# Two transposes in one visit, a block-diagonal inverse product, padded tiles and a reordered opening in a fused attention and gated-MLP kernel

## Chip, cores and metric

The kernel runs on one core of a Trainium2 chip. Five engines run their own queues: TensorE (PE; its weight loads are listed as PEld), VectorE (DVE), ScalarE (ACT), GpSimd (POOL) and SyncE (SP), which here issues the transfers. The metric is the device time of one launch in microseconds (us); lower is better. Matmuls read SBUF, the on-chip memory of 128 partitions, and write PSUM, eight banks of 2 KB per partition.

## What is computed

Landmark (Nyström) attention over 8 batches of 8 heads, followed by RMS normalisation and a gated MLP whose weights arrive in float64. Cut to what matters:

```python
q_lm = q.reshape(B, H, 32, 18, D).mean(axis=3)      # B=8, H=8, S=576, D=64
k_lm = k.reshape(B, H, 32, 18, D).mean(axis=3)
A, Bm, C = sm(q, k_lm), sm(q_lm, k_lm), sm(q_lm, k)  # softmax rows
Z = Bm.T / (norm1(Bm) * norminf(Bm) + 1e-6)
for _ in range(6):
    Z = 2 * Z - Z @ Bm @ Z
x = (A @ Z @ C @ v)                                  # -> 4608 tokens x 512
xn = x / sqrt(mean(x * x) + 1e-6) * rms_g
out = (silu(xn @ w_gate) * (xn @ w_val)) @ w_out     # d_ff = 1536
```

## The kernel before, in words

**The MLP** is the bulk of the work. For each batch it runs twice, over the first six blocks of 128 hidden columns ("early" weights) for batches 0 to 7, then over the last six ("late" weights) for batches 0 to 7. One such pass is 144 matmuls into `psg` and `psv` (moving operand: `an`, the normalised activations split into a high and a low part, 288 columns) and then 72 or 90 matmuls into `pso` (stationary: `h`; moving: `whio`/`wloo` early, `lhio`/`lloo` late, 512 columns). The weights are folded with each batch's attention values: `mix_weights` multiplies `WT` (from the inverse) with a pair of decoded weight blocks `wgv` into `pM`, and ACT and DVE split that into `Mhi` and `Mlo`. There are three pairs for each half.

**Decoding** turns a float64 block into float32: two ACT operations (L175, L178), two on DVE (L180, L183); out-weights need two more, `whio` on ACT and `wloo` on POOL. The first six raw blocks land in the `h` tiles, the later ones in a ring of three buffers, so that the transfer of the tenth block waits until the seventh has been decoded. A pair takes four blocks, gate and value of two hidden blocks.

**Attention** of the next batches is cut into short pieces, "visits", that stand between MLP matmuls at positions written in the code (`until(chunk, n)` counts MLP matmuls; `rest` and `steady` hold the tables). For each batch and each of two groups of four heads: landmark sums `lmT` (L380, DVE), `front` (scores `sC`, `sA`), `soften`, `turn` (transposes of `E` into `sE`, `sF`, copied to `ET`, `EL` by ACT) and `values` (`pCV`). Then come the inverse (`newton_start`, first product `p`, six steps `pn`, L668), `newton_weights` (eight small products `pW` with 32x32 blocks, copied twice side by side to `W`), `newton_values` (two transposes `pT`, scaled to `WT`), and `second` (`pO`, squares, `pss`, `pms`, the reciprocal root in small DVE steps, `an`). PSUM has four banks for the MLP (`pg`) and four for attention (`pa`). Each engine runs its queue in order; the order is made by the builder from these positions and priorities.

**The opening** (batch 0's attention, with no MLP work yet, then the first pass, in which batch 1's attention and the decoding of all early weights run too) has its own pieces: `opening`, `first_inverse`, `first_second`, and the head of `steady`. Batch 1's first `front` stands after batch 0's `pms` and first `pM`; batch 1's sums for its second group stand ahead of the second pair's decoding. In the first pass a pair is mixed in the middle of the pair before it (`very`).

**Layout.** `gsb`, the norm weights, takes 16 bytes a partition and is followed on the left side of SBUF by `WT`, the `h` tiles, early weights, `Mhi`, `Mlo`, `an` and others. In the built program these start 32 bytes past a multiple of 64; the late out-weights (on the right side) start at multiples of 64.

## Time and profile before

| | |
|---|---|
| Median of 3 runs | 837.14 us (836.75 to 837.6) |
| Profiled execution | 836.84 us |
| its span, first to last instruction | 834.7 us |
| TensorE busy | 800.4 us, 96% |
| VectorE busy | 490.9 us, 59% |
| ScalarE busy | 350.9 us, 42% |
| GpSimd busy | 71.0 us, 9% |
| Mean granted TensorE clock | 0.973 |

In the profile, a row of the timeline gives start, duration, engine, line, operation, output and inputs, and in brackets how long the engine sat idle before it and what ended that. A granted clock of 1.00 is 2.4 GHz and of 0.50 is 1.2 GHz. Matmul durations overlap, so that pitch is read from start to start. A float32 matmul that isn't a transpose shows as two instructions.

### The profile page before, as it was taken

Reading aid. Unit: us, or ns where it says so; the run is one execution under the profiler, and the core shown is the slowest. Engines: PE = TensorE matmul, PEld = TensorE weight load, DVE = VectorE, ACT = ScalarE, POOL = GpSimd, SP = SyncE. Lnnn points to the kernel's source line nnn. Section 1 sums busy time; section 2 is a strip of 40 time slices with the busy share of each in tenths; the row PEclk is TensorE's granted clock in tenths of the full one; section 3 lists DMA queues with packets and bytes.
Section 4 is the critical chain, followed back from the end, with each engine's and each line's share of the span. In section 5 each row is a group of like instructions: output and inputs, shape, how many; then the busy total and the mean of one; then the engine's idle time right before and its main releaser. Section 6 shows DMA issues by size and latency. Waiting matters only on the chain.

```text
span 834.7 us, 17401 instructions
## 1 busy us (share of the span) xinstructions
PE 800.4 (96%) x7192; PEld 630.3 (76%) x7192; DVE 490.9 (59%) x1095; ACT 350.9 (42%) x749; POOL 71.0 (9%) x97
## 2 busy tenths in 40 slices
PE   7756999999999999999999999999999999999998
PEld 4334667877878778777787879797979797979796
DVE  7787976856768748668584945242524252425241
ACT  4557644535445444445464844141414141414140
POOL 1012411020020200201110110000000000000000
PEclk8579999999999999999999999999999999999999
DMA  9756452250440612503436510413141304130202
GB/s 326 242 172 216 143 191 89 84 195 15 144 136 2 228 65 92 188 2 109 140 114 229 176 71 13 145 54 118 22 146 53 121 22 147 50 124 14 88 14 75
DMA packets 41054, 95.49 MB, mean 114 GB/s; under 512 B 4112, under 2 KB 17424, under 8 KB 38928
## 3 DMA queue, kind: packets, MB, share of 16 engines
q1 hardware_dynamic: 40976, 94.39, 33.4%
q8 instruction: 56, 0.92, 0.5%
q14 instruction: 22, 0.18, 0.1%
HBM read 66.06 MB, written 28.31 MB: 113 GB/s over the span
## 4 chain that ended last, share of the span: by engine, by line
PE 86%; DVE 5%; DMA 4%; ACT 2%; POOL 1%; issue 1%; SPq 1%; ACTq 0%; DVEq 0%
PE pso L109 35%; PE psg L109 19%; PE psv L109 18%; PE pM L109 6%; PE pn L109 2%; DMA wrawg<-in_moe_w_gate_dram 2%; PE pO L109 1%; PE sC L109 1%; PE pss L109 1%; DMA wrawv<-in_moe_w_val_dram 1%; PE pCV L109 1%; DMA qk<-in_k_dram 1%; PE sE L112 1%; DVE wgv L180 1%; SPq L152 0%
## 5 line engine op out<-in xcount | busy, mean ns | idle before, releaser
L109 PE MATMUL pso<-whio,h 128*128 128x512 f32 x432 | 140.7, 397 | 2.1 <-ACT ob L848 2.1
L109 PE MATMUL pso<-lhio,h 128*128 128x512 f32 x432 | 138.7, 396 | 0.0
L316 DVE TENSOR_TENSOR s<-s,psv 128x288 f32<-128x288 f32 x192 | 85.9, 450 | 60.0 <-PE psv L109 59.3
L315 ACT ACTIVATE s<-psg 128x288 f32<-128x288 f32 x192 | 78.7, 410 | 89.9 <-PE psg L109 89.5
L268 ACT CAST Mhi<-pM 128x512 fp32r<-128x512 f32 x96 | 51.4, 591 | 137.6 <-PE pM L109 137.2
L323 ACT CAST h<-s 128x576 fp32r<-128x576 f32 x96 | 64.6, 673 | 86.2 <-DVE s L316 86.2
L109 PEld LDWEIGHTS pso<-whio,h 128*128 128x128 f32 x432 | 81.6, 189 | 24.3 <-issue 4.2
L109 PEld LDWEIGHTS pso<-lhio,h 128*128 128x128 f32 x432 | 81.0, 187 | 24.8 <-DVE obl L911 5.9
L324 DVE TENSOR_TENSOR h<-s,h 128x576 fp32r<-128x576 f32 x96 | 72.7, 758 | 44.5 <-ACT h L323 44.3
L109 PE MATMUL psg<-an,Mhi 128*128 128x288 f32 x384 | 85.4, 307 | 4.8 <-ACT s L315 3.4
L911 DVE TENSOR_TENSOR obl<-obl,pso 128x512 f32<-128x512 f32 x36 | 24.8, 688 | 107.6 <-PE pso L109 107.4
L109 PE MATMUL pso<-wloo,h 128*128 128x512 f32 x216 | 86.4, 400 | 0.0
L109 PE MATMUL pso<-lloo,h 128*128 128x512 f32 x216 | 85.2, 395 | 0.0
L109 PE MATMUL psv<-an,Mhi 128*128 128x288 f32 x384 | 84.4, 303 | 0.0
L270 DVE TENSOR_TENSOR Mlo<-pM,Mhi 128x512 fp32r<-128x512 f32 x94 | 60.3, 683 | 37.5 <-ACT Mhi L268 37.5
L109 PE MATMUL psg<-anl,Mhi 128*128 128x288 f32 x384 | 81.7, 301 | 0.6 <-DVE Mlo L270 0.6
L109 PE MATMUL psv<-anl,Mhi 128*128 128x288 f32 x384 | 79.1, 294 | 0.0
L109 PEld LDWEIGHTS psg<-an,Mhi 128*128 128x128 f32 x384 | 62.3, 191 | 17.5 <-issue 6.7
L109 PEld LDWEIGHTS psg<-anl,Mhi 128*128 128x128 f32 x384 | 60.9, 188 | 15.5 <-issue 12.6
L109 PEld LDWEIGHTS psv<-an,Mhi 128*128 128x128 f32 x384 | 61.6, 188 | 6.1 <-issue 2.2
L109 PEld LDWEIGHTS psv<-anl,Mhi 128*128 128x128 f32 x384 | 61.5, 188 | 0.0
L109 PE MATMUL psg<-an,Mlo 128*128 128x288 f32 x192 | 58.5, 305 | 0.0
(138 smaller groups left out, 1249.8 us busy)
## 6 DMA issues: line engine op xcount, KB each, us to landing
qk<-in_q_dram SPq DMA_DIRECT2D x16, 576.0 KB, 4.8
qk<-in_k_dram SPq DMA_DIRECT2D x16, 576.0 KB, 5.8
ad<-an SPq DMA_DIRECT2D x8, 1152.0 KB, 5.1
pd<-ob SPq DMA_DIRECT2D x36, 256.0 KB, 2.4
anl<-ad SPq DMA_DIRECT2D x8, 1152.0 KB, 5.1
obl<-pd SPq DMA_DIRECT2D x36, 256.0 KB, 2.7
out_dram<-obl SPq DMA_DIRECT2D x36, 256.0 KB, 2.0
vt<-in_v_dram SPq DMA_DIRECT2D x16, 512.0 KB, 4.1
```

The costliest lines, as they stand in the source:

```text
L109: tc.keep_in_program_order(nc.tensor.matmul(*args, **kw))
L112: tc.keep_in_program_order(nc.tensor.transpose(*args))
L180: nc.vector.scalar_tensor_tensor(w, w, 3, wtail, op0=ALU.logical_shift_left, op1=ALU.bitwise_or)
L268: nc.scalar.copy(hi[:, g], ps[g])
L270: nc.vector.tensor_sub(lo[:, g], ps[g], hi[:, g].bitcast(F32))
L315: silu["last"] = nc.scalar.activation(s[:, cols], banks[0], AF.Silu).ins
L316: nc.vector.tensor_mul(s[:, cols], s[:, cols], banks[1])
L323: nc.scalar.copy(h[:, 0, TAIL:], s)
L324: gated[b, f0 // NF1, 2 * n + i] = nc.vector.tensor_sub(h[:, 1, TAIL:], s, h[:, 0, TAIL:].bitcast(F32))
L911: nc.vector.tensor_add(ob, ob, ps)
```

## The change

1. **Tiles.** `gsb` is padded to 64 bytes. In the built program the left-side tiles then start at multiples of 64; those on the right side stay where they were.
2. **Inverse product.** `newton_weights` and `newton_values` become one visit. GpSimd copies the four 32x32 blocks of each group into a block-diagonal 128x128 matrix `blocks` (four copies a batch); two matmuls with it give `pW` straight (for `W`, now half as wide) and two give it turned, which DVE scales to `WT`. `VF` is written by two DVE instructions instead of one.
3. **Reciprocal root.** Eight DVE steps instead of ten.
4. **Visits of batches 2 to 7.** Both `turn`s in one visit, both `values` and the first inverse product in the next, `ET` and `EL` with two buffers; positions moved.
5. **Opening.** Batch 1's first sums stand ahead of `WT`; its first `front` stands between batch 0's `pms` and the first `pM`; one more weight block is decoded before `an`; batch 1's second sums stand behind the decoding of two pairs; the next pair is mixed half a block later, behind 12 more MLP matmuls; the remaining positions moved.

```diff
-    gsb = cst.tile([P, NK], F32, name="gsb")
+    gsb = cst.tile([P, 16], F32, name="gsb")[:, :NK]
     WT = cst.tile([P, B, NK, 2 * M], F32, name="WT")
+    blocks = cst.tile([P, 2, P], F32, name="blocks")
+    nc.gpsimd.memset(blocks, 0.0)
...
             for i in range(2):
-                if very and i and n + 1 < NPAIR:
-                    mix_weights(wts, b, pairs[n + 1])
-                    yield 1.1
                 s = mp.tile([P, S], F32, name="s", tag="s", bufs=2)
                 for e in range(2):
+                    if very and i and e and n + 1 < NPAIR:
+                        mix_weights(wts, b, pairs[n + 1])
+                        yield 1.1
...
             yield from until(*next(at))
-            values(b, 0)
-            turn(b, 1)
+            if b > 1:
+                turn(b, 0)
+                turn(b, 1)
+                yield 1.1, 0.0
+                yield from until(*next(at))
+                values(b, 0)
+                values(b, 1)
+            else:
+                values(b, 0)
+                turn(b, 1)
+                yield 1.5, 0.0
+                yield from until(*next(at))
+                values(b, 1)
...
-            front(1, 0, fixed["an", 0].ins)
-            load_qk(2, 0)
-            yield 1.3, 0.0
-            sums(1, 1, fixed["mx", 1, 0].ins)
-            yield from until(0, 24)
+            yield from until(0, 12)
             turn(1, 0)
             yield 0.65, 0.0
-            yield from until(0, 36)
+            yield from until(0, 37)
+            sums(1, 1, early.last)
+            yield from until(0, 46)
             front(1, 1)
...
-            at = [46, 58, 70] + [78 + 8 * n for n in range(6)] + [126, 132, 138, n_gv + 4, n_gv + 10, n_gv + 18]
+            at = [54, 66, 78] + [84 + 7 * n for n in range(6)] + [126, 136, n_gv + 4, n_gv + 10, n_gv + 18]
...
-                enter = [n_gv + n for n in ((4, 28, 36, 48, 54, 66) if c else (16, 40, 46, 56, 62, 70))]
+                enter = [n_gv + n for n in ((4, 30, 44, 50, 62) if c else (16, 40, 52, 60, 70))]
...
-                after = [7 * n for n in range(7)] + [48, 54, 68, 86, 96]
+                after = [7 * n for n in range(6)] + [48, 56, 68, 86, 96]
...
+            for h in range(4):
+                nc.gpsimd.tensor_copy(blocks[rows(h), :, rows(h ^ 1)], Bs[rows(h)])
+            return BT, den
...
-            for g in range(2):
-                for h in range(4):
-                    r = rows(rho(g, h))
-                    mm(pW[rows(pos(g, h)), g], Bs[r, g, :], VF[r, g, :], start=True, stop=True)
-            W = sm.tile([P, 2, 2, D], F32, name="W", tag="W", bufs=2)
-            fixed[b] = nc.vector.tensor_copy(W, pW.unsqueeze(2).broadcast_to([P, 2, 2, D]))
+            for g in range(2):
+                mm(straight[:, g], blocks[:, g], VF[:, g, 0], start=True, stop=True)
+            for g in range(2):
+                mm(turned[:, g], VF[:, g].rearrange("p a d -> p (a d)"), blocks[:, g], start=True, stop=True)
+            W = sm.tile([P, 2, D], F32, name="W", tag="W", bufs=1)
+            fixed[b] = nc.vector.tensor_copy(W, straight)
...
-            for n, took in enumerate(second(0)):
-                yield took
-                if n == 2:
-                    low_parts = mix_weights(early, 0, 0, True)
-                    yield 1.1, 0.0
+            parts = second(0)
+            yield next(parts)
+            sums(1, 0, fixed[0].ins)
+            yield next(parts)
+            yield from parts
+            front(1, 0, fixed["r1", 0].ins, fixed["an", 0].ins)
+            load_qk(2, 0)
+            yield 1.3, 0.0
+            low_parts = mix_weights(early, 0, 0, True)
+            yield 1.1, 0.0
             low_parts()
```

How the order changes is shown at three places. The first is DVE in the opening. Before, behind the score transposes `tA` of batch 1's first group (numbers behind a name tell tiles apart; `wgv_664` is the second pair):

```order
L440 STREAM_TRANSPOSE tA<-sA 128x288 x2
L380 TENSOR_REDUCE lmT<-qk_353 128x64 x2
L180 SCALAR_TENSOR_TENSOR wgv_664<-wgv_664,wrawg_356 128x4x128
L433 TENSOR_SCALAR ss<-ss 128x1
L434 TENSOR_SCALAR ss<-ss 128x1
L183 SCALAR_TENSOR_TENSOR wgv_664<-wrawg_356,wgv_664 128x4x128
L435 RECIPROCAL rs<-ss 128x2
L316 TENSOR_TENSOR s<-s,psv 128x288
```

Now, at the end of the same decoding (`wgv_554` is the second pair, `wgv_755` the third; the second pair's first block was decoded ahead of `an`):

```order
L182 SCALAR_TENSOR_TENSOR wgv_554<-wgv_554,wrawv_366 128x4x128
L319 TENSOR_TENSOR s<-s,psv 128x288
L327 TENSOR_TENSOR h_713<-s,h_713 128x576
L185 SCALAR_TENSOR_TENSOR wgv_554<-wrawv_366,wgv_554 128x4x128
L182 SCALAR_TENSOR_TENSOR wgv_755<-wgv_755,wrawg_368 128x4x128
L185 SCALAR_TENSOR_TENSOR wgv_755<-wrawg_368,wgv_755 128x4x128
L383 TENSOR_REDUCE lmT<-qk_357 128x64 x2
L273 TENSOR_TENSOR Mlo<-pM,Mhi 128x512 x2
```

The landmark sums `lmT` of batch 1's second group moved from ahead of the second pair's decoding to behind it and behind the third pair's first block.

The second place is TensorE in the second pass, where batch 2's inverse ends. Before:

```order
L109 MATMUL psg<-an,Mhi 128x288 x2
L109 MATMUL psg<-an,Mlo 128x288
L109 MATMUL pW<-VF,Bs 32x64 x8
L109 MATMUL psv<-an,Mhi 128x288 x2
L109 MATMUL psv<-an,Mlo 128x288
L109 MATMUL psv<-an,Mhi 128x288 x2
L109 MATMUL psv<-an,Mlo 128x288
L112 MATMUL pT<-ident,W 128x128 x2
L109 MATMUL pM<-wgv_743,WT 32x512 x8
```

Now:

```order
L111 MATMUL psg<-an,Mhi 128x288 x2
L111 MATMUL psg<-an,Mlo 128x288
L111 MATMUL psv<-an,Mhi 128x288 x2
L111 MATMUL psv<-an,Mlo 128x288
L111 MATMUL psv<-an,Mhi 128x288 x2
L111 MATMUL psv<-an,Mlo 128x288
L111 MATMUL pW<-VF,blocks 128x64 x2
L111 MATMUL pW<-blocks,VF 128x128 x2
L111 MATMUL pM<-wgv_755,WT 32x512 x8
```

The two visits `pW` and `pT` became one, of four full-width matmuls, just ahead of `pM`.

The third place is ACT at the end of the first pass, around the copies `ob` that free the banks of `pso`. Before:

```order
L739 ACTIVATE sq<-pO 128x288 x2
L424 ACT_TABLE_LOAD
L424 ACTIVATE E,ss<-sC,mx 128x288
L774 CAST an<-AT 128x576 x2
L424 ACTIVATE E,ss<-sC,mx 128x288
L428 ACTIVATE eb,ss<-sC,mx 128x32
L848 COPY ob<-pso 128x512 x2
L268 CAST Mhi<-pM 128x512 x2
```

Now:

```order
L191 CAST whio_1221<-w_1216 128x512
L775 CAST an<-AT 128x576 x2
L859 COPY ob<-pso 128x512 x2
L427 ACT_TABLE_LOAD
L427 ACTIVATE E,ss<-sC,mx 128x288 x2
L431 ACTIVATE eb,ss<-sC,mx 128x32
L271 CAST Mhi<-pM 128x512 x2
```

The `ob` copies moved from behind batch 2's exponentials `E` to ahead of them.

## Rows read from the trace of the kernel before

**Rows 1.** Busy time by stage (engine busy us and count, then TensorE's granted clock).

```profile
40.00:60.00 20.00, 10.78 (x97) 6.19 (x89) 17.68 (x42) 10.80 (x20) 3.09 (x1) 0.76 0.41 144
60.00:80.00 20.00, 13.67 (x213) 10.24 (x205) 15.35 (x45) 13.87 (x28) 3.72 (x4) 0.93 0.70 228
80.00:100.00 20.00, 19.48 (x234) 14.40 (x222) 17.22 (x33) 14.06 (x30) 9.16 (x8) 0.94 0.44 137
...
140.00:800.00 660.00, 658.90 (x5689) 530.48 (x5688) 370.20 (x804) 268.94 (x576) 44.85 (x68) 1.00 0.29 99
```

**Rows 2.** TensorE's waits: total us, times, longest us.

```profile
PE pM L109 <- DVE wgv L183: 7.5, 1, 7.5
...
PE psg L109 <- ACT s L315: 3.4, 2, 2.9
PE pso L109 <- ACT ob L848: 2.1, 1, 2.1
```

**Rows 3.** Timeline from 36 to 60 us: start, us, engine, line, operation [idle before].

```profile
42.07 1.07 ACT L276 CAST Mlo<-pM 128x512 fp32r<-128x512 f32 x2 [0.40 <-PE pM L109]
...
48.88 2.57 DVE L380 TENSOR_REDUCE lmT<-qk 128x64 f32<-128x1152 f32 x2
...
51.37 0.68 DVE L180 SCALAR_TENSOR_TENSOR wgv<-wgv,wrawg 128x512 int32<-128x512 int32 x1
...
56.32 3.09 POOL L322 CAST h<-h 128x128 fp32r<-128x128 f32 x1 [37.79 <-DVE h L324]
...
57.97 0.68 DVE L183 SCALAR_TENSOR_TENSOR wgv<-wrawv,wgv 128x512 int32<-128x512 int32 x1
...
58.71 1.96 PE L109 MATMUL pM<-wgv,WT 64*32 64x512 f32 x16 [7.52 <-DVE wgv L183]
```

**Rows 4.** Timeline from 60 us, VectorE's two waits for weights.

```profile
61.76 0.69 DVE L180 SCALAR_TENSOR_TENSOR wgv<-wgv,wrawv 128x512 int32<-128x512 int32 x1 [2.50 <-ACT wgv L178]
...
65.84 0.69 DVE L180 SCALAR_TENSOR_TENSOR wgv<-wgv,wrawg 128x512 int32<-128x512 int32 x1 [2.65 <-ACT wgv L178]
```

**Rows 5.** Timeline, two out-matmuls: the first of all, and one that waited.

```profile
97.05 0.40 PE L109 MATMUL pso<-whio,h 128*128 128x512 f32 x1
...
115.08 0.50 PE L109 MATMUL pso<-whio,h 128*128 128x512 f32 x1 [2.08 <-ACT ob L848]
```

**Rows 6.** Chain of work, two long runs of out-matmuls: start, us, what and count.

```profile
475.98 20.42 PE pso L109 x90
...
810.12 20.97 PE pso L109 x90
```

**Rows 7.** Timeline of batch 5's attention visits, TensorE, between out-matmuls.

```profile
276.87 0.60 PE L112 MATMUL sE<-ident,E 128*128 128x128 f32 x4
277.30 0.27 PE L112 MATMUL sF<-ident,E 128*64 128x128 f32 x1
...
287.20 0.48 PE L109 MATMUL pso<-whio,h 128*128 128x512 f32 x1
287.52 0.39 PE L109 MATMUL pso<-wloo,h 128*128 128x512 f32 x1
```

**Rows 8.** Timeline, TensorE, matmuls around a pW and around a pT visit.

```profile
94.02 0.29 PE L109 MATMUL psv<-an,Mlo 128*128 128x288 f32 x1
...
94.72 0.29 PE L109 MATMUL psg<-an,Mlo 128*128 128x288 f32 x1
...
249.78 0.30 PE L109 MATMUL psg<-an,Mlo 128*128 128x288 f32 x1
...
250.19 0.29 PE L109 MATMUL psg<-an,Mlo 128*128 128x288 f32 x1
...
251.15 0.29 PE L109 MATMUL psv<-an,Mlo 128*128 128x288 f32 x1
```

**Rows 9.** Tile h: durations min/median/max of the tail copies on GpSimd.

```profile
L322 POOL CAST h<-h x48: 289/293/3088, 56.3 to 772.6; 128x128 fp32r<-128x128 f32 x48
```

More of the change, by code (lines that the diff above doesn't have):

```diff
@@ L130, in __init__ @@
             self.place = place
-            self.spots, self.ahead, self.after, self.then = spots, ahead, None, None
+            self.spots, self.ahead, self.after, self.then, self.last = spots, ahead, None, None, None
             self.raws, self.gv, self.out = {}, {}, {}
@@ L182, in load_next @@
                 )
-            nc.vector.scalar_tensor_tensor(
+            last = nc.vector.scalar_tensor_tensor(
                 w, whead, -0x80000000, w, op0=ALU.bitwise_and, op1=ALU.bitwise_or
             )
+            self.last = last.ins
             if nm == "o":
@@ L385, in sums, with front @@
                     )
-        def front(b, g, after=None):
+        def front(b, g, after=None, late=None):
             nt, lmT, qk = state[b], lms.pop((b, g)), loaded.pop((b, g))
@@ L447, in front @@
             if b:
-                tail(after)
+                tail(late or after)
             return tail
@@ L531, in rest @@
             yield from until(*next(at))
-            values(b, 0)
-            turn(b, 1)
+            if b > 1:
[11 more added lines that the diff above has]
+                values(b, 1)
             if b + 1 < B:
                 load_v(b + 1, 0)
-            yield 1.5, 0.0
-            yield from until(*next(at))
-            values(b, 1)
-            if b + 1 < B:
                 load_v(b + 1, 1)
@@ L552, in rest @@
             with tc.high_priority():
-                newton_weights(b, inverse[2])
-            yield 0.4, 0.0
-            yield from until(*next(at))
-            with tc.high_priority():
-                newton_values(b)
-            yield 0.3, 0.0
+                newton_weights(b)
+            yield 0.6, 0.0
             stage["newton"] = stage["wt"] = b
@@ L603, in steady @@
                 yield from until(c, enter[1])
-                turn(b, 0)
-                yield 0.65, 0.0
-                yield from until(c, enter[2])
                 front(b, 1)
@@ L611, in steady @@
                 inverse = newton_start(b)
-                after = [7 * n for n in range(7)] + [48, 54, 68, 86, 96]
-                yield from rest(b, inverse, [(c, n) for n in enter[3:]] + [(c + 1, n) for n in after])
+                after = [7 * n for n in range(6)] + [48, 56, 68, 86, 96]
+                yield from rest(b, inverse, [(c, n) for n in enter[2:]] + [(c + 1, n) for n in after])
         def bmm(lt, rhs, n, nm):
@@ new lines, in newton_weights @@
+            for g in range(2):
+                mm(turned[:, g], VF[:, g].rearrange("p a d -> p (a d)"), blocks[:, g], start=True, stop=True)
+            W = sm.tile([P, 2, D], F32, name="W", tag="W", bufs=1)
+            fixed[b] = nc.vector.tensor_copy(W, straight)
+            fixed["WT", b] = nc.vector.tensor_mul(
+                WT[:, b],
+                turned.rearrange("p g (j n) -> p (g j) n", j=2),
+                gsb.unsqueeze(2).broadcast_to([P, NK, 2 * M]),
+            )
+            state[b]["W"] = W
@@ L706, in newton @@
                 yield 0.45, NP
[L707 to L710 removed]
+            newton_weights(b)
+            yield 0.6, WW
             stage["wt"] = b
@@ L735, in second @@
                         r = rows(pos(g, h))
-                        mm(po[2 * g + h // 2][half(h)], W[r, g, 0, :], ATs[g][r, cols], start=True, stop=True)
+                        mm(po[2 * g + h // 2][half(h)], W[r, g, :], ATs[g][r, cols], start=True, stop=True)
                 sq = ap.tile([P, NK, HS], F32, name="sq", tag="sq", bufs=2)
@@ L757, in second @@
             r2 = sm.tile([P, NB], F32, name="r2", tag="r2")
-            ri = r1.bitcast(I32)
-            nc.vector.tensor_single_scalar(ri, ms.bitcast(I32), 1, op=ALU.logical_shift_right)
-            nc.vector.tensor_scalar(ri, ri, -1, 0x5F3759DF, op0=ALU.mult, op1=ALU.add)
-            for c in (1.0, RS):
-                nc.vector.tensor_mul(r2, r1, r1)
-                nc.vector.scalar_tensor_tensor(r2, r2, c, ms, op0=ALU.mult, op1=ALU.mult)
-                nc.vector.scalar_tensor_tensor(r2, r2, -10.0 / 3.0, r2, op0=ALU.add, op1=ALU.mult)
-                last = nc.vector.scalar_tensor_tensor(r1, r2, 5.0, r1, op0=ALU.add, op1=ALU.mult)
+            nc.vector.tensor_scalar(
+                r1.bitcast(I32), ms.bitcast(I32), -0.5, 0x5F3759DF, op0=ALU.mult, op1=ALU.add
+            )
+            nc.vector.tensor_mul(r2, r1, r1)
+            nc.vector.scalar_tensor_tensor(r2, r2, -0.5, ms, op0=ALU.mult, op1=ALU.mult)
+            nc.vector.scalar_tensor_tensor(r1, r2, 1.5, r1, op0=ALU.add, op1=ALU.mult)
+            nc.vector.tensor_mul(r2, r1, r1)
+            nc.vector.tensor_mul(r2, r2, ms)
+            nc.vector.scalar_tensor_tensor(r2, r2, -10.0 / 3.0, r2, op0=ALU.add, op1=ALU.mult)
+            last = nc.vector.scalar_tensor_tensor(r1, r2, 5.0, r1, op0=ALU.add, op1=ALU.mult)
+            fixed["r1", b] = last
             if b == 0:
@@ L814, in nystrom_moe_kernel @@
         new_state(0)
+        new_state(1)
         if WN0:
@@ L832, in decode @@
             yield from early.stream(WAIT0, NEAR)
+            while ("sums", 1) not in fixed:
+                yield -0.3
+            early.then = fixed["sums", 1].ins
+            yield from early.stream(WAIT0, 1)
         early.ahead, early.after = 2, fixed["eb", 0, 1].ins
```

41 lines of the change are left out of this document (14 added, 27 removed).

## The prediction, made before the changed kernel was run

> **What bounds the kernel now.** I read the busy time by stage first. From 140 to 800 us TensorE is busy 658.90 of 660 us at a granted clock of 1.00 (2.4 GHz) [rows 1]: there nothing that another engine does can be won back, and only the number, the pitch or the gaps of TensorE's own instructions count. Between 40 and 100 us it is busy 10.78, 13.67 and 19.48 of 20 us, that is 16.07 us idle, and the granted clock is 0.76, 0.93 and 0.94 [rows 1]. In the same 60 us DVE is busy 17.68 + 15.35 + 17.22 = 50.25 us, so DVE has 9.75 us left: it is the engine that nearly binds the opening. The second view is TensorE's waits: one of 7.5 us for the second weight pair's last decoding step (L183), 2.9 of 3.4 us for `s` on ACT, 2.1 us for a copy `ob` on ACT [rows 2]. The third is the timeline there: DVE first sums landmarks (`lmT`, 2.57 us), begins to decode the second pair at 51.37 and writes its last step at 57.97; TensorE starts `pM` at 58.71 [rows 3]. Then DVE waits 2.50 and 2.65 us itself for further raw weights [rows 4]. So the kernel is a steady part set by TensorE's pitch, and an opening set by DVE's order.
>
> **Opening.** The wait of 7.5 us ends with DVE's row of work. Three things leave that row: the `lmT` pair, 2.57 us [rows 3]; the two steps of the pair's first block, which now fall into DVE's idle time ahead of `an`, 2 x 0.68 = 1.36; and one step of the third pair that stood ahead of the second pair's last, another 0.6 (a step lasts 0.68 [rows 3], and they follow one another a little closer). That is 4.5 us. Against it, the second cast of `an` now stands on ACT behind the two `Mlo` casts (1.07 us together [rows 3]), and DVE's `an` and the decoding wait for that: 4.5 - 1.1 = 3.4 us. Ahead of the second pair's `pM` there are now 12 more matmuls `psg`/`psv`, which did not wait for it and used to come after it: 3 such in 250.19 - 249.78 = 0.41 us [rows 8], so 12 take 1.6. TensorE is then 3.4 + 1.6 = 5.0 us ahead at the same work. The moved `lmT` does not come back as a loss, since it lands where DVE waited 2.50 us [rows 4]. The raw blocks behind it are asked for sooner, because the ring's buffers come free sooner; the other DVE wait, 2.65 us [rows 4], and TensorE's wait of 2.9 us for `s`, which lies behind it on ACT [rows 2], then shrink. I take 2.0 us of that, since ACT still has the same casts and decodings to do. Together -7.0 us at the first `pso`, which was at 97.05 [rows 5]. The bounds: -9.75, all of DVE's idle time [rows 1], and -2, if ACT's queue eats the 12 matmuls and the early block. Earlier `front`, shorter root and the earlier sums are inside this: they only move DVE steps of a fixed total and lie beside the casts that `an` waits for.
>
> **End of the first pass.** The `ob` copies now precede batch 2's exponentials, so the wait of 2.08 us at 115.08 [rows 5] goes. What is late next is batch 2's second `front`, placed 6 out-matmuls earlier; its `lmT` pair (2.57 us [rows 3]) stands behind `an` of batch 1 on DVE, whereas the four banks and the whole queue of TensorE stand behind that `front`. I put the new wait at 2.1 us, so that the two cancel; bounds 0 and 2.6, by the same row.
>
> **Batches 2 to 7.** Two visits in place of three. After a visit the next `pso` starts 287.52 - 287.20 = 0.32 us after the first one behind it [rows 7], where two follow each other in 20.42 / 90 = 0.227 [rows 6]: 0.09 us lost on leaving; I take as much for entering, 0.18 a batch, 6 x 0.18 = -1.1. The doubled `ET` copies on ACT have some 12 out-matmuls of cover, 2.7 us; if ACT's `tA` steps eat it, the cost is at most one more such copy, for which a 512-column step of 0.68 us [rows 3] is the nearest row: up to 0.7 a batch, kept for the range.
>
> **Inverse product.** Before, the `pW` visit costs 251.15 - 250.19 - 0.41 = 0.55 and `pT` 94.72 - 94.02 - 0.41 = 0.29 [rows 8], 0.84 together. Now there are four full-width float32 matmuls, which show as eight instructions, each with a 128-column weight load. Nearest are the transposes `sE`: four in 277.30 - 276.87 = 0.43 [rows 7], 0.11 each. Eight take 0.86, with 0.09 for leaving 0.95: +0.1 a batch, for seven batches inside the stream +0.7. The halved `W` and the second `VF` step are on DVE, which has time left there. Bounds -0.3 and +1.5 for all.
>
> **Tiles.** Early out-matmuls run at 20.42 / 90 = 0.2269 us, late ones at 20.97 / 90 = 0.2330 [rows 6], with the same shape and clock. What differs is the place: early `h` and `whio` both start 32 bytes past a multiple of 64, late `h` still does but `lhio` starts at a multiple. After the change all start at multiples. If it is the disagreement of the two operands that costs, the late ones drop to the early pitch: 2 x 324 = 648 late matmuls x 0.0061 = -3.9 us, and nothing else changes. I take this, because the one pair of rows that shows a difference has equal offsets on the fast side. The other ends are in the rivals. The Trainium skill speaks against any gain: "SBUF — State Buffer", section "Operand start alignment", asks only that an operand start at a multiple of its element size and names no better start. By that the term would be 0 and the sum 3.9 us higher; no run here shows it yet, and the two pitches have then another cause.
>
> **The sum.** 836.84 (profiled execution) - 7.0 + 0 - 1.1 + 0.7 - 3.9 = 825.5. The median stands 0.3 above the profiled execution, so 825.8.
>
> **Rivals.** *Pitch unchanged*: the late pitch comes from something else (copies, stores), the padding does nothing: 829.7. For it speaks that the late half also has other users of the memory; against it that 90 undisturbed matmuls at the end keep it [rows 6]. *All matmuls gain*: the slow thing is a start off 64 bytes anywhere: 648 early `pso` and 2304 `psg`/`psv` gain up to 0.0061 each, 18 us more: 808 to 822. Against it: early `pso`, off 64 on both sides, is the faster one. *A start at 64 bytes is the slow one* (slower side): what marks the slow late rows is a moving operand at a multiple of 64. Then early `pso` go to the late pitch, 648 x 0.0061 = +4.0, the late ones stay, and `psg`/`psv`, whose `an` moves to such a start too, may gain as much: 2304 x 0.0061 = +14. That gives 836.84 - 7.4 + 4.0 = 833.7 without them and 847.8 with them; it is slower than before once `psg`/`psv` cost over 0.0015 us more each. For it speaks the same pair of rows [rows 6], which can't tell the two readings apart. *The opening's gain is lost*: the four `blocks` copies run on GpSimd among DVE's decoding, and one GpSimd copy took 3.09 us at 56.32 between such steps [rows 3] where the median is 0.293 [rows 9]; with the casts queued behind `Mlo` this eats the 7 us: 832.8, up to 835.4 if the new `front` wait comes on top. Against it: `blocks` are wanted only six steps later. The Trainium skill's "SBUF — State Buffer", section "Who interferes with whom", says that a DVE instruction with two SBUF inputs blocks a GpSimd one that reads SBUF; the copy's 3.09 us agrees.
>
> **Chances.** The sum as it stands 0.45 (821 to 830); pitch unchanged 0.21 (826 to 834); all gain 0.07; slow start 0.13 (half of it above 838); opening lost 0.10 (832 to 837); none of these 0.04. The range 815 to 836 leaves out most of "all gain" and of the slow start. About 0.2% is what a measurement of this kernel can tell from no change, 835.5 to 838.8 here: faster 0.83, same 0.07, slower 0.10, from the upper half of the slow start and the worst of the others.
>
> **What would show it.** Right: the wait for L183 falls from 7.5 us to about 2 or less, the first `pso` stands near 90, late runs of 90 `pso` take 20.4 us, and no row of `psg` changes. Wrong: a 90-run early at 20.97; `psg` groups of 3 over 0.41; a wait of `sC` for `lmT` over 3 us near 115; `pCV` waits for `ET` in every batch; or a first `pso` after 94, which would leave the opening to ACT's queue.

## The result, and the profile after

The changed kernel takes 828.37 us (median of 4 runs, 828.0 to 829.41); beside it the kernel before took 836.94 us (median of 4, 834.67 to 837.6). The ratio is 0.9904, with an interval from 0.9884 to 0.9925: 8.6 us faster by the medians, where 11.3 were forecast. The profiled execution took 828.0 us with a span of 826.2 us, 8.5 less than the span before (834.7).

Where the 8.5 us came from is seen by cutting both spans at the same four points of the program. In the trace they are the first out-matmul `pso`, the 73rd (the first of the second pass), the first one of the late half, and the last one. All are read at the start of the matmul.

| stretch | before, us | after, us | difference | forecast |
|---|---|---|---|---|
| start to the first `pso` | 97.05 | 94.46 | -2.59 | -7.0 |
| first `pso` to the second pass's first | 62.29 | 59.02 | -3.27 | 0 |
| from there to the first late `pso` | 360.11 | 360.93 | +0.82 | -0.4 |
| late half, to the start of the last `pso` | 311.23 | 307.75 | -3.48 | -3.9 |
| sum | 830.68 | 822.16 | -8.52 | -11.3 |

The sum is near the forecast, but only the term of the late half is: the opening gave little over a third of what was expected, the end of the first pass gave 3.3 us that were not expected at all, and the third stretch lost 0.8 us where 0.4 were to be gained. That the errors partly cancel (4.4, 1.2 and 0.4 us too little, 3.3 too much) is luck.

The busy time by stage, which answers [rows 1] (columns: stretch, us; busy us and count of TensorE, its weight loads, VectorE (DVE), ScalarE (ACT), GpSimd (POOL); granted clock, DMA share, GB/s):

```profile
40.00:60.00 20.00, 15.30 (x131) 9.43 (x124) 15.05 (x40) 9.78 (x22) 0.62 (x1) 0.75 0.41 146
60.00:80.00 20.00, 16.33 (x221) 11.66 (x220) 19.93 (x51) 16.17 (x30) 6.89 (x9) 0.76 0.74 233
80.00:100.00 20.00, 19.42 (x216) 14.30 (x209) 19.75 (x33) 14.56 (x31) 9.10 (x9) 0.98 0.44 149
140.00:800.00 660.00, 658.89 (x5627) 536.76 (x5627) 369.11 (x797) 267.55 (x577) 49.85 (x88) 1.00 0.29 99
```

From 140 to 800 us nothing has changed in kind: TensorE is busy 658.89 of 660 us. In the opening it is now busy 4.5 us more between 40 and 60 us and 2.7 more from 60 to 80, there in part because the granted clock is lower (0.76 for 0.93) and the same matmul lasts longer. But look at DVE: it has 4.95 us left in the first of these stretches, more than before (2.32), and 0.07 and 0.25 us in the other two. The idle time of DVE that the prediction wanted to use from 60 us on is used up; what is left stands ahead of 60 us.

TensorE's waits, which answer [rows 2] (us in total, times, longest):

```profile
PE pM L111 <- DVE wgv L185: 1.9, 1, 1.9
...
PE psg L111 <- ACT s L318: 1.4, 2, 0.9
```

The wait for the second pair's last decoding step (L183 before, L185 now) went from 7.5 to 1.9 us, the wait for `s` from 3.4 to 1.4, and the wait for `ob` is gone. A reader who stops here would call the opening's forecast right. The timeline says otherwise. Rows that answer [rows 3] and [rows 5] (start, us, engine, line, operation, then the idle time before it and what ended it):

```profile
46.26 0.67 ACT L775 CAST an<-AT 128x576 fp32r<-128x576 f32 x1 [6.58 <-DVE AT L773]
46.84 1.06 ACT L271 CAST Mhi<-pM 128x512 fp32r<-128x512 f32 x2
...
48.00 1.08 ACT L279 CAST Mlo<-pM 128x512 fp32r<-128x512 f32 x2
...
48.97 0.67 ACT L775 CAST an<-AT 128x576 fp32r<-128x576 f32 x1
49.68 0.76 DVE L776 TENSOR_TENSOR an<-AT,an 128x576 fp32r<-128x576 f32 x1 [1.77 <-ACT an L775]
...
55.36 0.46 DVE L319 TENSOR_TENSOR s<-s,psv 128x288 f32<-128x288 f32 x1 [1.03 <-PE psv L111]
...
56.93 0.46 DVE L319 TENSOR_TENSOR s<-s,psv 128x288 f32<-128x288 f32 x1 [0.52 <-PE psv L111]
...
58.71 1.09 PE L111 MATMUL pM<-wgv,WT 64*32 64x512 f32 x16 [1.89 <-DVE wgv L185]
...
94.46 0.40 PE L111 MATMUL pso<-whio,h 128*128 128x512 f32 x1
```

The second pair's `pM` starts at 58.71 us, exactly where it started before [rows 3]. The shorter wait only means that TensorE did something else meanwhile: the 12 `psg`/`psv` that used to come behind. The second cast of `an` stands behind both `Mhi` and `Mlo` on ACT, DVE waits for it, and its second `an` ends at 49.68 + 0.76 = 50.44 us. Before, both stood one behind the other and ended at 45.74 + 1.43 = 47.17:

```profile
45.74 1.43 DVE L775 TENSOR_TENSOR an<-AT,an 128x576 fp32r<-128x576 f32 x2
```

The chain of work, two long runs of out-matmuls (start, us, what, count), for [rows 6]:

```profile
470.94 20.42 PE pso L111 x90
...
802.13 20.44 PE pso L111 x90
```

The late runs are now as fast as the early ones: 20.44 / 90 = 0.2271 us a matmul, where it was 20.97 / 90 = 0.2330. The early runs kept 20.42. This is what the forecast for the tiles said, almost to the digit.

### The profile page after: what moved, and what is told of

The parts are those of the page before. It is cut to its first block, busy times and chain, and to the rows that moved or that the text cites. A ratio compares the mean times of both kernels' runs of the same rounds, so it can differ in the third digit from the quotient of the medians.

```text
span 826.2 us, 17288 instructions
## 1 busy us (share of the span) xinstructions
PE 797.0 (96%) x7112; PEld 635.1 (77%) x7112; DVE 492.9 (60%) x1087; ACT 349.6 (42%) x749; POOL 78.2 (9%) x130
## 4 chain that ended last, share of the span: by engine, by line
PE 88%; DVE 4%; DMA 4%; ACT 2%; issue 1%; SPq 1%; ACTq 0%; DVEq 0%
PE pso L111 36%; PE psg L111 19%; PE psv L111 18%; PE pM L111 6%; DMA wrawg<-in_moe_w_gate_dram 2%; PE pn L111 2%; PE sC L111 2%; PE pO L111 1%; PE pCV L111 1%; PE pss L111 1%; DMA qk<-in_k_dram 1%; SPq L154 1%; PE sE L114 1%; PE pW L111 1%; DVE h L327 1%
## 5 line engine op out<-in xcount | busy, mean ns | idle before, releaser
L111 PE MATMUL pso<-lhio,h 128*128 128x512 f32 x432 | 136.5, 392 | 0.0
L327 DVE TENSOR_TENSOR h<-s,h 128x576 fp32r<-128x576 f32 x96 | 74.4, 775 | 42.0 <-ACT h L326 41.5
L111 PE MATMUL psv<-an,Mlo 128*128 128x288 f32 x192 | 59.2, 308 | 0.0
```

The costliest lines, as they stand in the source:

```text
L111: tc.keep_in_program_order(nc.tensor.matmul(*args, **kw))
L327: gated[b, f0 // NF1, 2 * n + i] = nc.vector.tensor_sub(h[:, 1, TAIL:], s, h[:, 0, TAIL:].bitcast(F32))
```

## The experiments

Each ratio is against runs of the kernel before on the same chip. Small differences between kernels of the opening are read from traces: one execution differs from the next there by up to 1.3 us. Four of the profiles below have the changed kernel's opening in the same order (after, its second profile g0_after_again, a1, a4), with the first `pso` at 94.46, 95.26, 95.29 and 95.04 us; three have the old one (before, a2, a3), at 97.05, 96.28 and 97.60. By these averages the opening gained 2.0 us; the -2.59 of the table is one pair.

### What makes the late out-matmul slow

The forecast took the disagreement of the two operands' places; the rivals were that any start off 64 bytes costs, that a start at 64 bytes costs, and that the padding does nothing. Four kernels set the places one by one.

a1_gsb16, the change without the padding of the left side:

```
-    gsb = cst.tile([P, 16], F32, name="gsb")[:, :NK]
+    gsb = cst.tile([P, NK], F32, name="gsb")
```

> The changed kernel with the norm weights' tile back at 16 bytes, so that the left-side tiles start 32 bytes past a multiple of 64 again and the late out-weights stay at multiples. If operands that start at different places within 64 bytes cost time: the last 90 out-matmuls take 20.97 us again (20.44 in the changed kernel), the early 90 stay at 20.42, and the time is 648 x 0.0059 = 3.8 us above the changed kernel's 828.4, 832.2. If the late pitch fell for another reason: 20.44 and 828.4.

a2_before_gsb64, the kernel before with that padding alone:

```
-    gsb = cst.tile([P, NK], F32, name="gsb")
+    gsb = cst.tile([P, 16], F32, name="gsb")[:, :NK]
```

> The kernel before with the tile padded to 64 bytes and nothing else. If the place within 64 bytes is the cause: the last 90 take 20.44 us, nothing else changes, 836.9 - 3.8 = 833.1. If it needs another part of the change: 20.97 and 836.9. If psg and psv gain too (all starts now at multiples of 64): 48 of them take less than their 6.36 us.

a3_before_right32, the kernel before with a pad of another size on the right side, so that all starts lie 32 bytes past a multiple of 64:

```
-    al.tile([P, 8], F32, name="pad")
+    al.tile([P, 16], F32, name="pad")
```

> The kernel before with the spacer on the right side at 64 bytes instead of 32: the late out-weights then start 32 bytes past a multiple of 64, like h. If only the two operands' disagreement costs: the last 90 take 20.44 us with no start at a multiple of 64 anywhere, and 833.1. If multiples of 64 are what makes it fast: 20.97 or more, and 836.9 or more.

a4_after_right32, the same pad in the changed kernel, so that `h` lies at a multiple of 64 and the late weights 32 bytes past one:

> The changed kernel with the same spacer: h at a multiple of 64, the late out-weights 32 bytes past one, the opposite disagreement to that of the kernel before. If any disagreement costs: the last 90 take 20.97 us, 832.2. If only h off a multiple of 64 (with the weights on one) costs: 20.44, 828.4.

Measured: a1 831.84 us (ratio 0.9951, 0.9932 to 0.9969), a2 832.10 (0.9955, 0.9937 to 0.9973), a3 832.65 (0.9957, 0.9942 to 0.9972), a4 831.64 (0.9947, 0.9928 to 0.9966). The early and the late run of 90 in the chain of work of a1:

```profile
471.78 20.42 PE pso L111 x90
...
805.90 20.97 PE pso L111 x90
```

and of a3:

```profile
475.01 20.42 PE pso L109 x90
...
806.20 20.44 PE pso L109 x90
```

a2 shows 20.42 and 20.44 as a3 does, and a4 20.42 and 20.97 as a1 does. So the late run is fast with both operands at a multiple of 64 (after, a2) and with both 32 bytes past one (a3), and slow with either one of them there and the other not (before and a1 in one sense, a4 in the other). It is the disagreement that costs, 0.2330 - 0.2271 = 0.0059 us a matmul; the multiple of 64 itself is worth nothing. That rules out "all matmuls gain" and "a start at 64 bytes is the slow one" along with "pitch unchanged". Nor do `psg` and `psv` gain: the stretch from the second pass's first `pso` to the first late one, which is full of them, takes 360.11 us before, 360.17 in a2 and 360.10 in a3. Only differences of 0 and 32 bytes were tried. By whole times the padding is worth 836.74 - 832.10 = 4.6 us on the kernel before and 3.7 on the changed one (831.84 - 828.12, a1 and g0, on the same chip); the traces give 3.5 in the late half (311.23 - 307.75).

The prediction set against this the Trainium skill's page "SBUF — State Buffer", section "Operand start alignment". That section asks for a multiple of the element size and adds that this concerns legality, not speed, so that it speaks neither for nor against a gain. The runs agree with the first (every one of these starts is taken), and they show a price of the relative place, 0.2330 against 0.2271 us.

### What holds the opening back

b2_old_product takes the old inverse product (32-row pieces, two visits) into the changed kernel:

```
-            for g in range(2):
-                mm(straight[:, g], blocks[:, g], VF[:, g, 0], start=True, stop=True)
...
+                for h in range(4):
+                    r = rows(rho(g, h))
+                    mm(pW[rows(pos(g, h)), g], Bs[r, g, :], VF[r, g, :], start=True, stop=True)
...
-                after = [7 * n for n in range(6)] + [48, 56, 68, 86, 96]
+                after = [7 * n for n in range(7)] + [48, 56, 68, 86, 96]
```

> The changed kernel with the old inverse product: eight small products, one VF step, W copied twice side by side, two transposes in a visit of their own, no blocks copies. In the changed kernel the copy of batch 0's W starts at 32.58 us (30.70 before) and the first MLP matmul at 48.29 (45.76 before). Per batch the new product costs 0.12 us more on TensorE, so the steady part gains 0.7 us. If the slower product at the half clock is what delays the opening: W near 30.7, first MLP matmul near 46.9 and first out-matmul near 93.2 (94.46), 826.5 in all. If the opening is set by what VectorE and ScalarE have to do from 60 to 95 us: first out-matmul within 0.5 of 94.5, and 827.7.

c3_pm_first puts the first pair's casts ahead of both casts of `an` again, as before, and the first `front` behind them:

```
-            yield from parts
-            front(1, 0, fixed["r1", 0].ins, fixed["an", 0].ins)
...
+            yield next(parts)
             low_parts = mix_weights(early, 0, 0, True)
             yield 1.1, 0.0
+            yield from parts
             low_parts()
             yield 0.5, 0.0
+            front(1, 0, fixed["r1", 0].ins, fixed["an", 0].ins)
```

> The changed kernel with batch 0's first pM and the subtraction of its high part back ahead of batch 1's first front, so that the casts Mhi and Mlo come before those of an on ScalarE. If the casts queued ahead of the second an cast delay the opening: the first MLP matmul starts 1.5 to 2.3 us earlier than 48.29, and the first out-matmul as much earlier: 826.1 to 826.9. If VectorE's work from 60 to 95 us binds: the first MLP matmul comes earlier, but the first out-matmul within 0.5 us of 94.46: 828.4.

b2 ran 826.80 us (0.9885, 0.9865 to 0.9906), c3 826.79 (0.9884, 0.9864 to 0.9904); both intervals overlap that of the change, so each alone is not told from it by whole times. The traces tell the mechanism. The product in the kernel after (TensorE, then DVE's copy of it):

```profile
30.49 1.08 PE L111 MATMUL pW<-VF,blocks 128*128 128x64 f32 x4 [0.50 <-DVE VF L669]
31.37 1.17 PE L111 MATMUL pW<-blocks,VF 128*128 128x128 f32 x4
32.58 0.29 DVE L684 COPY W<-pW 128x128 f32<-128x128 f32 x1 [0.83 <-PE pW L111]
32.92 1.25 PE L111 MATMUL pO<-AT,W 32*64 32x288 f32 x10 [0.39 <-DVE W L684]
```

and in the kernel before, up to the second stage's `pO`:

```profile
29.97 0.65 PE L109 MATMUL pW<-VF,Bs 32*32 32x64 f32 x16 [0.41 <-DVE VF L668]
30.70 0.42 DVE L678 COPY W<-pW 128x256 f32<-128x256 f32 x1 [0.18 <-PE pW L109]
31.18 0.69 PE L112 MATMUL pT<-ident,W 128*128 128x128 f32 x2 [0.56 <-DVE W L678]
31.80 1.89 PE L109 MATMUL pO<-AT,W 32*64 32x288 f32 x16
```

The copy that batch 0's second stage waits for starts 1.88 us later: 0.52 of it is there before the product starts, and the product itself takes 2.05 us in place of 0.65 (granted clock 0.50 from 30 to 33 us in both). But the two `pT` transposes that used to stand between copy and `pO` are gone, so `pO` starts only 32.92 - 31.80 = 1.12 us later. A part of that may be an avoidable wait: the copy reads the first two products (over at 31.57 us) and yet waits 0.83 us for the turned ones in the same PSUM tile; no run took that away. In b2 the copy is back at 30.99 and DVE's second `an` at 48.74 (after: 49.68), 0.94 us sooner. In c3 both `an` follow one another on DVE from 48.12, without the wait of 1.77 us between them, and the second starts at 48.79, 0.89 sooner; the first MLP matmul comes at 47.93, only 0.4 us sooner and not the 1.5 to 2.3 of that reading. The second pair's `pM` starts at 58.70 (b2) and 58.11 (c3), against 58.71 to 59.43 in the four unchanged openings, and the first `pso` gained only -0.49 (b2, 94.77) and -1.14 (c3, 94.12) on the 95.26 of g0: b2 lies within the spread of the four, c3 0.3 below it.

c2_sums_early puts the landmark sums of batch 1's second group back ahead of the second pair's decoding (between the two `an`, where before they stood behind both):

```
+            sums(1, 1, fixed["mx", 1, 0].ins)
             yield from until(0, 12)
...
-            yield from until(0, 37)
-            sums(1, 1, early.last)
```

> The changed kernel with the landmark sums of batch 1's second group (2.6 us on VectorE) ahead of the second pair's decoding again, between the two steps of an. If the place of these sums was the gain that I forecast: the second pair's pM starts about 2.6 us later than 58.71, and the first out-matmul comes 1 to 2.6 us later, 829.5 to 831. If VectorE's whole work binds: the sums now fill 1.77 us in which VectorE waited for the second an cast, pM starts about 0.8 us later, what lies behind is earlier by the rest, and the first out-matmul stays within 0.5 us or comes up to 1 earlier, 827.5 to 828.9.

It ran 833.72 us (0.9970, 0.9960 to 0.9980), 5.4 us above the change, more than either theory gave. Its timeline, TensorE and DVE:

```profile
60.42 1.09 PE L111 MATMUL pM<-wgv,WT 64*32 64x512 f32 x16 [1.89 <-DVE wgv L185]
...
69.82 1.17 PE L114 MATMUL sE<-ident,E 128*128 128x128 f32 x4 [1.93 <-ACT E L427]
...
74.55 0.85 PE L111 MATMUL psg<-an,Mhi 128*128 128x288 f32 x2 [1.90 <-ACT s L318]
...
99.14 0.39 PE L111 MATMUL pso<-whio,h 128*128 128x512 f32 x1
```

`pM` comes 1.71 us later, and the waits behind it are then longer than in the change: DVE 1.43 us for raw weights, TensorE for `E` and for `s`. The first `pso` is 4.7 us late (3.9 against g0). So the later sums are the part of the opening that gained. That they gained more than their own 2.57 us because they are out of the way of decoding and also fill DVE's wait for raw weights is argued from these waits: in c2 the builder, which makes the order anew from the positions, also put other steps of DVE and ACT behind 60 us in another order, and no run parts the two. The other half of the reading is as useful: with the sums early, the changed opening is 99.14 - 97.05 = 2.1 us worse than the old one. That this is the price of the product and of the split of the two `an` casts is likely, and f1 below measures that price.

### Whether GpSimd's turn at the memory costs

In the changed kernel two DVE steps of the opening take twice their usual time, each beside a multiplication of `tA` on GpSimd (POOL):

```profile
75.56 1.16 POOL L472 TENSOR_TENSOR tA<-tA,rA 128x576 f32<-128x576 f32 x1 [3.94 <-DVE rA L470]
75.69 1.57 DVE L182 SCALAR_TENSOR_TENSOR wgv<-wgv,wrawv 128x512 int32<-128x512 int32 x1
...
80.29 1.35 DVE L327 TENSOR_TENSOR h<-s,h 128x576 fp32r<-128x576 f32 x1
```

c4_weigh_dve does batch 1's two multiplications on DVE:

```
-            eng = nc.gpsimd if b else nc.vector
+            eng = nc.gpsimd if b > 1 else nc.vector
```

> The changed kernel with batch 1's two row scalings of tA on VectorE instead of GpSimd (two steps of about 0.75 us more for VectorE, two of 1.2 to 1.4 less for GpSimd). From 60 to 96 us seven VectorE instructions last 5.1 us longer than such ones do elsewhere, each while a GpSimd instruction runs. If GpSimd holds VectorE up: the two long ones beside these scalings (1.57 us at 75.69, 1.35 at 80.29) fall to 0.68 and 0.75, so VectorE loses nothing by taking the work over, and the first out-matmul is within 0.5 us of 94.46 or earlier. If the long ones have another cause: they stay, VectorE has 1.5 us more to do, and the first out-matmul comes about 1.5 us later, 829.9.

e1_no_scale leaves them out:

```
-            eng.tensor_mul(tA, tA, rA.unsqueeze(2).broadcast_to([P, NB, M]))
+            if b != 1:
+                eng.tensor_mul(tA, tA, rA.unsqueeze(2).broadcast_to([P, NB, M]))
```

> The changed kernel without the row scaling of batch 1's tA (left out: two GpSimd instructions of 1.2 and 1.4 us; batch 1 then goes through the MLP unscaled). VectorE's own work is as in the changed kernel. If those two hold VectorE up and VectorE binds from 60 to 95 us: its instructions near 76 and 80 us fall from 1.57 and 1.35 to about 0.7 us each, and the first out-matmul comes 1 to 1.5 us earlier than in the changed kernel. If they do not bind: those instructions get shorter, but the first out-matmul stays within 0.5 us of 94.46.

c4 ran 830.07 us (0.9925, 0.9904 to 0.9946), with the first `pso` at 96.22: both long steps are normal, but the two multiplications stand in DVE's row (0.79 and 0.74 us) and TensorE waits 2.7 us for the inverse's `PV` (2.0 in the change). e1 ran 829.71 (0.9925, 0.9908 to 0.9941). Its timeline:

```profile
76.26 0.68 DVE L182 SCALAR_TENSOR_TENSOR wgv<-wgv,wrawv 128x512 int32<-128x512 int32 x1
...
79.62 0.75 DVE L327 TENSOR_TENSOR h<-s,h 128x576 fp32r<-128x576 f32 x1
...
95.00 0.39 PE L111 MATMUL pso<-whio,h 128*128 128x512 f32 x1
```

With nothing on GpSimd beside them the same steps take 0.68 and 0.75 us, so 1.49 us are taken off DVE, and the first `pso` comes at 95.00 against 95.26 in g0: nothing that can be told from no change. The lock-out is shown; that its price is not on the path is only argued, because e1 changes more than that. With the two instructions gone, the builder put other steps of DVE and ACT in another order from 74 us on, and the whole kernel is 1.6 us slower than g0 on the same chip (829.71 and 828.12, no execution of one within the range of the other). The trace has that loss behind the first `pso`: 60.80 us to the second pass against 58.99, most of it in the visit of `pO`, which waits for ACT's squares, and these stand behind a decoding step that waited 1.97 us for GpSimd's `wloo`. The Trainium skill's "SBUF — State Buffer", section "Who interferes with whom", describes an exclusive lock between these two engines; the 1.57 against 0.68 us agree with it.

### Where the end of the first pass gained

d1_ob_late holds the first two `ob` copies behind batch 2's exponentials, as before:

```
-            nc.scalar.copy(ob, ps)
+            with tc.issue_after(fixed["eb", 2, 0].ins) if t < 2 else nullcontext():
+                nc.scalar.copy(ob, ps)
```

> The changed kernel with the first two copies ob held behind batch 2's exponentials on ScalarE, as in the kernel before. There TensorE's gap at the third weight visit pM of the first pass cost 3.37 us against 1.22 in the changed kernel, and the 5 out-matmuls and the visits after it ran at half the clock. If the place of the copies makes that gap: it returns, TensorE waits about 2 us for ob near 110 and out-matmuls behind it are 0.427 apart for some us, and the stretch from the first out-matmul to the second pass is 2 to 3 us longer than the changed kernel's 59.02. If the gap came from something else (fewer decodings left on ScalarE by then): that stretch stays within 0.5 us.

It ran 832.96 us (0.9963, 0.9949 to 0.9977). Timeline of TensorE behind its `pM` visit, and the stretch around it (columns as above):

```profile
114.34 0.80 PE L111 MATMUL pso<-whio,h 128*128 128x512 f32 x1 [3.49 <-ACT ob L860]
...
115.37 1.05 PE L111 MATMUL pso<-whio,h 128*128 128x512 f32 x2
```

```profile
109.00:120.00 11.00, 7.51 (x73) 4.24 (x72) 9.04 (x22) 6.23 (x16) 0.00 (x0) 0.84 0.55 206
```

The same place in the kernel after:

```profile
107.00:118.00 11.00, 9.85 (x87) 6.37 (x86) 10.82 (x29) 7.32 (x20) 1.27 (x2) 1.00 0.83 307
```

In d1 a pair of out-matmuls behind the wait takes 1.05 us, at a granted clock of 0.84 over 11 us; in the change the clock is 1.00 there and a pair takes 0.62 (114.56). Before, the wait of 2.08 us [rows 5] was followed by pairs of 1.05 too:

```profile
117.14 1.05 PE L109 MATMUL pso<-whio,h 128*128 128x512 f32 x2
```

From the first `pso` to the second pass's first d1 needs 62.01 us (95.89 to 157.90), 3.0 more than the change (59.02) and about what the kernel before needed (62.29). So the place of the `ob` copies makes that wait, and in d1 the half clock (1.2 in place of 2.4 GHz) behind it. But these are not the same 3.0 us that the change gained. A visit is priced here as the time from the start of the last `pso` ahead of it to the start of the second `pso` behind it, less two pitches of 0.227. The `pM` visit costs 5.04 us in d1, where the wait is 3.49, but cost 3.37 before; the next visit then gives 1.2 back. And the visit of `pO`, which cost 2.71 before, costs 0.95 in d1 as in the change, so that this part of the gain has nothing to do with the copies. `pO` before, which waited for squares on ACT, and in d1:

```profile
98.51 2.13 PE L109 MATMUL pO<-AT,W 32*64 32x288 f32 x16 [0.37 <-ACT sq L739]
```

```profile
96.90 0.82 PE L111 MATMUL pO<-AT,W 32*64 32x288 f32 x16
```

Nor does the half clock follow such a wait every time. a3 has the first pass of the kernel before, in the same order, and waits as long for `ob`, but its granted clock stays at 1.00 from 116 to 120 us (0.65 and 0.50 in the two halves of that stretch before):

```profile
115.65 0.50 PE L109 MATMUL pso<-whio,h 128*128 128x512 f32 x1 [2.07 <-ACT ob L848]
...
117.47 0.62 PE L109 MATMUL pso<-whio,h 128*128 128x512 f32 x2
```

Its stretch takes 60.79 us, against 62.29 before and 62.33 in a2; that of the changed first pass takes 58.97 to 59.02 in four profiles. So of the 3.3 us that the stretch gained, about 1.5 are a half clock that one execution of the old kernel shows and another does not.

### A kernel from what was learned

f1_best takes b2 and c3 together, and places batch 3's and the later batches' second `front` at 36 again, where `pM` stands, with the visits behind it moved along:

```
-                enter = [n_gv + n for n in ((4, 30, 44, 50, 62) if c else (16, 40, 52, 60, 70))]
+                enter = [n_gv + n for n in ((4, 36, 48, 54, 66) if c else (16, 40, 52, 60, 70))]
```

> The changed kernel with three parts put right at once: the old inverse product (0.12 us less TensorE time a batch), batch 0's first pM ahead of batch 1's first front, and, for batches 3 to 7, the second front back at out-matmul 36, beside pM, where both together cost 2.40 us instead of 1.39 + 1.23. If the visit costs add: 6 x 0.1 + 5 x 0.22 = 1.7 us less in the steady part, and up to 0.5 in the opening: 1.7 to 2.2 us below the changed kernel. If the later second front makes a batch's values wait for ET: waits at pCV, and less than 0.8 us below it.

Beside it the change was run again, unedited:

> The changed kernel itself, on the same chip as the next one, as its measure: 0.9904 of the kernel before by the first measurement, so 828.4 by 836.9.

f1 ran 824.05 us (823.48 to 824.85), ratio 0.9857 (0.9841 to 0.9874); g0 828.12, ratio 0.9907 (0.9890 to 0.9923). The intervals don't overlap: f1 is 4.1 us faster than the change, about twice the 1.7 to 2.2 expected, and beats both kernels. Its timeline, the opening and the visit in batch 3:

```profile
45.98 1.42 DVE L778 TENSOR_TENSOR an<-AT,an 128x576 fp32r<-128x576 f32 x2
...
55.92 1.09 PE L109 MATMUL pM<-wgv,WT 64*32 64x512 f32 x16 [1.89 <-DVE wgv L183]
...
91.63 0.40 PE L109 MATMUL pso<-whio,h 128*128 128x512 f32 x1
...
216.56 0.39 PE L109 MATMUL pso<-whio,h 128*128 128x512 f32 x1
...
219.41 0.40 PE L109 MATMUL pso<-wloo,h 128*128 128x512 f32 x1
```

With the product short and the casts in the old order, DVE's `an` ends 3.0 us sooner than in the change, `pM` starts 2.8 us sooner, and from `pM` to the first `pso` it takes 35.71 us as in the change (35.75). Against g0, whose `pso` was at 95.26, the gain is 3.6 us (2.8 against the earliest of the four unchanged openings), while b2 alone gave 0.5 and c3 alone 1.1. Two waits stood one behind the other, and taking away one left the other: b2 keeps DVE's wait of 1.78 us between the two `an`, c3 keeps the late copy of `W` (32.49 us). From the second pass's first `pso` to the first late one f1 needs 359.16 us, 1.8 less than the change.

The visit of the second `front` and of `pM` shows most of that 1.8. Priced as above, in f1, where the two share one entry: 219.41 - 216.56 - 0.454 = 2.40. In the change they are apart:

```profile
218.56 0.39 PE L111 MATMUL pso<-whio,h 128*128 128x512 f32 x1
...
220.41 0.39 PE L111 MATMUL pso<-wloo,h 128*128 128x512 f32 x1
...
221.33 0.40 PE L111 MATMUL pso<-whio,h 128*128 128x512 f32 x1
...
223.02 0.40 PE L111 MATMUL pso<-wloo,h 128*128 128x512 f32 x1
```

220.41 - 218.56 - 0.454 = 1.40, and 223.02 - 221.33 - 0.454 = 1.24, together 2.63. The kernel before had 229.06 - 226.21 - 0.454 = 2.40 for both in the same batch:

```profile
226.21 0.39 PE L109 MATMUL pso<-whio,h 128*128 128x512 f32 x1
...
229.06 0.40 PE L109 MATMUL pso<-wloo,h 128*128 128x512 f32 x1
```

So five batches of the stretch lose 0.23 each, and the old product gives back about 0.5 (b2 needs 360.43 us for the stretch, the change 360.93).

## Why the prediction was right in sum and wrong in three terms

**Opening: the term was too large, and the step that failed is the delay of `an`.** The prediction let 4.5 us leave DVE's row ahead of the second pair's last decoding step and set 1.1 against them for the `an` cast behind `Mlo`. The 4.5 did leave: nine decoding steps and the `lmT` pair stood between `an` and `pM` before, six steps now. But the second `an` ended 50.44 - 47.17 = 3.27 us later, not 1.1. Two causes stand behind that: the product, which was called +0.1 a batch inside the stream and nothing here, and the casts, `Mhi` as well as `Mlo`. Undone alone, the product gives back 0.94 us of it (b2) and the order of the casts 0.89 (c3); undone together they give 50.44 - 47.40 = 3.04 (f1). Behind it DVE now waits 1.03 and 0.52 us for `psv`, whose 12 matmuls run while the granted clock is 0.67 (50 to 55 us). 4.5 - 3.27 - 1.55 = -0.3: `pM` starts where it did, at 58.71. The sum's second part, 1.6 us for those 12 matmuls now done ahead, can stay as it stands, and 2.59 - 1.6 = 1.0 us is left for everything behind, where 2.0 were expected (and 0.4, if the 2.0 us of all profiles stand for 2.59): DVE is full from 60 us on, and TensorE's granted clock from 60 to 80 us is 0.76 where it was 0.93 [rows 1]. Which of the two takes the missing 1.0, no run tells apart. f1 shows the delay of `an` to be the cause by undoing it: the first `pso` comes 2.8 to 3.7 us sooner.

The sizing of the product was the avoidable mistake. It was taken from `sE` transposes in the steady stream [rows 7], 0.11 us each at full clock. In the opening the granted clock is 0.50 from 30 to 33 us, and there the eight instructions took 2.05 us, with batch 0's second stage waiting behind them.

**End of the first pass: right that the wait for `ob` goes, wrong in what it is worth.** Priced as above, the `pM` visit went from 3.37 to 1.22 us, the 2.1 of [rows 2]. The new wait came as foreseen, at the second `front` of batch 2: that visit costs 3.25, 1.36 more than the same `front` cost before and 1.86 more than it costs in a later batch, against 2.1 forecast. What the forecast did not have are two other things. The half-clock pitch from 116.6 to 119.4 us is gone (-0.8, and a part of the `front` before); a3 shows that this was not sure to be there. And the visit of the second stage's `pO` fell from 2.71 to 0.96, those of transposes and values from 3.62 to 3.23, while `pms` with the `front` beside it went from 1.52 to 2.55. d1 shows that the `pM` visit hangs on the `ob` copies, and that the `pO` visit does not; what made `pO` cheaper is open, and is read off the rows only as ACT's squares coming earlier.

**Batches 2 to 7: -1.1 + 0.7 forecast, +0.8 measured.** Both sized parts held: transposes and values of a batch 3.37 to 3.22 us, -0.15 (forecast -0.18), the inverse product 1.99 to 2.11, +0.12 (forecast +0.1). Missing was a part of the change that the prediction passed over: the second `front` moved from 36 to 30 and so no longer shares its entry with `pM`, +0.23 a batch. By sum that is +0.2 a batch and +1.0 for the five batches of the stretch, against +0.82 measured. f1 undoes it and gets it back.

**Tiles: right,** -3.48 against -3.9, by the mechanism given, with the four combinations of a1 to a4 behind it. The chance of 0.21 for "pitch unchanged" and 0.13 for the slow start were the price of having one pair of rows.

**Rivals.** "The opening's gain is lost" was half of what happened, for another reason than the one it gave: `psg` waited for the casts as it said, but taking a part of GpSimd's lock-out away made the first `pso` no earlier (e1). Of the signs that were named beforehand, the late runs at 20.44 told rightly. The wait for L183 fell to 1.9 as it should, without the gain that it stood for, since `pM` started no sooner. "A first `pso` after 94" was said to leave the opening to ACT's queue. It was at 94.46; f1 confirms that reading together with the product, and c3, which mends the casts alone, is too near the spread to do so.

**Open.** The same opening varies by 0.8 us at the first `pso` between four profiles (94.46 to 95.29), so of c4's +1.0 over g0 little can be said, and b2's -0.5 and c3's -1.1 alone prove little without f1. The granted clock from 50 to 55 us is 0.67 in the change, 0.51 in g0, 0.56 in b2 and 0.92 in f1, so that a part of what b2 did not gain and f1 did may be the clock. Why c2 loses 4.7 us at the first `pso` where `pM` is only 1.7 late is argued from its waits, not shown by a run of its own.

## What to carry to other kernels

Price a step at the clock and with the cover of the place where it stands: what costs 0.1 us in a full stream can cost 1.1 at the head of a chain, and undoing one of two waits that stand in series shows little until both are undone. A wait that shrinks in the table of waits is no gain by itself; look whether the waiting instruction starts any sooner. Where visits to a stream are merged or moved, count for each neighbour whether it still shares an entry, and lay the two operands of a hot matmul at the same place modulo 64 bytes.

## What the runs showed of the hardware

- A 128x128 by 512 matmul whose moving operand and weights lie at places that differ by 32 bytes modulo 64 takes 0.2330 us in a long run, with equal places 0.2271, whether these are multiples of 64 or not (before, after, a1 to a4).
- A DVE step with two inputs took 1.57 in place of 0.68 us beside a GpSimd multiplication that itself lasted 1.16 (after and g0 against c4 and e1).
- The four full-width float32 products took 2.05 us in the opening, at a granted clock of 0.50. The old form took 0.65 for its 16 pieces and 0.69 for the two transposes in the same place.
- A wait of TensorE of 2.1 us (before, a2) or 3.5 us (d1) was followed by out-matmuls at the half clock, 0.43 in place of 0.227 us apart, for 1 to 3 us; the same wait of 2.07 us in a3 was not.
